# Moving a ring of four weight buffers by 64, 128, 192 and 256 bytes modulo 512 against the operand that streams through TensorE

## The chip, the cores and the metric

The kernel runs on one NeuronCore of one Trainium2 chip. The metric is the device time of one execution in microseconds. The kernel before took 2663.15 us as the median of two runs (2661.93 and 2664.38).

## What is computed

The input x is 8 sequences of 3008 tokens with 256 channels. Each sequence goes through a real Fourier transform along its tokens, a complex 256 x 256 mix of the channels, a soft threshold and the inverse transform; each token then goes through a gated feed-forward layer with 1536 hidden channels:

```python
X = np.fft.rfft(x, axis=1)
Yr = Xr @ w_r - Xi @ w_i + b_r
Yi = Xr @ w_i + Xi @ w_r + b_i
Y = soft(Yr, 0.01) + 1j * soft(Yi, 0.01)
x = np.fft.irfft(Y, n=3008, axis=1).reshape(8 * 3008, 256)
g = x @ w_gate
return (g / (1 + exp(-g)) * (x @ w_val)) @ w_out
```

## The kernel before

The work has two stages. The **transform stage** fills about the first 600 us: small matmuls (96x512, 128x128, 128x256, 128x512) compute the transforms and the mix, intermediate results go out to DRAM and come back, and the feed-forward weights are prepared and stored in DRAM. The **feed-forward stage** fills the rest. It runs over 24 blocks of tokens (22 of 2 x 512 tokens and 2 of 2 x 384), in each block over 6 pairs of hidden channels, and in each pair over gate and value: 24 x 6 x 2 = 288 steps, each a call of `gate_or_value`.

A step multiplies 2 x 2 blocks with seven products instead of eight (a Strassen-like scheme, with sums of blocks made by the other engines). Every operand is kept as two parts, an upper one rounded to fp32r and the rest, and `product` (L630 to L632) makes one product from three matmuls:

```python
for i, (w, x) in enumerate(((1, 0), (0, 0), (0, 1))):
    nc.tensor.matmul(o, lhsT=weights[w], rhs=parts[x], ...)
```

So one step has 7 x 3 = 21 matmuls of the "up" kind. Their stationary operand (lhsT, which TensorE loads before the matmul, the profile's LDWEIGHTS) is a 128 x 128 block of the step's weight unit `wup`, and their moving operand (rhs) is half of a tokens' part `x_parts`, 512 columns of 4 bytes in each partition. Among them stand "down" products of the pair before: the same `product`, with weights from `wdn_hi` and `wdn_lo`, which stay in SBUF throughout, and with `h_parts` as the moving operand. The order of the instructions of TensorE, VectorE, ScalarE and GpSimd is written out by hand in `gate_or_value`; on TensorE a run of 3, 6 or 9 "up" matmuls is followed by 3 "down" ones, over and over. In 32 steps `inverse` (L839 to L843) puts eight small fp32 matmuls in between, the end of the inverse transform of the last two sequences.

**The ring.** A weight unit has 2 x 7 x 128 floats in each partition (7168 bytes). `load_unit` (L586 to L590) takes the next of RING = 4 buffers of the pool `ring` and starts the DMA of a unit from DRAM on SP's queue; step k starts the load of unit k + 3 (L721). The pool is opened in `open_ring` (L582 to L584) at the right end of SBUF, behind a tile `pad` of PAD = 216 floats that nothing uses.

**Where the operands begin.** In this program the buffers of `wdn_hi`, `wdn_lo`, `x_parts` and `h_parts` all begin at 128 modulo 512 in each partition. A buffer of the ring takes 7168 = 14 x 512 bytes, and with the pad of 864 bytes above them all four ring buffers begin at 128 modulo 512 too (byte 199808, 206976, 214144 and 221312 of the partition). A block of weights is 512 bytes, a half of a tokens' part 2048. So for every matmul of the feed-forward stage the weights and the moving operand begin at the same place modulo 512. In the transform stage this differs: `f_hi` and `f_lo` begin 128 bytes above `wm_hi` and `wm_lo` modulo 512 (L366, L380), and `wi_hi` and `wi_lo` 128 bytes below `y_hi` and `y_lo` (L425).

Of the kernel before, what the change touches and what calls it, by code (L numbers as in the profile page):

```python
# [10 lines left out]
F32R = mybir.dt.float32r  # L11
# [6 lines left out]
P = 128  # L18
# [25 lines left out]
FIRST_X = {2: -0.93, 3: -0.90, 4: -0.5}  # L44
W_FIRST, W_STEP = 2, 4.2
WARM = 5
PAD = 216
GAPS = {1: (0.38,), 2: (0.38, 0.78), 3: (0.38, 0.78, 0.90), 4: (0.38, 0.40, 0.78, 0.90), 5: (0.36, 0.38, 0.40, 0.78, 0.90)}
AFTER = {0.36: 0.62, 0.38: 0.63, 0.40: 0.64, 0.78: 1.03, 0.90: 1.15}

# [59 lines left out]
def f32(ap):  # L110
    return ap.bitcast(F32)
# [458 lines left out]
class FFN:  # L570
# [11 lines left out]
    def open_ring(self):  # L582
        self.ctx.enter_context(self.tc.tile_pool(name="pad", bufs=1, side="right")).tile([P, PAD], F32, name="pad")
        self.ring = self.ctx.enter_context(self.tc.tile_pool(name="ring", bufs=RING, side="right", reuse_waits="tile"))  # L584

    def load_unit(self, k):  # L586
        if k >= len(BLOCKS) * len(self.units):
            return
        self.held[k] = self.ring.tile([P, 2, 7, P], F32R, name="wup")
        self.tc.nc.sync.dma_start(f32(self.held[k].rearrange("p i n a -> p i (n a)")), self.wup_d[self.units[k % len(self.units)]])  # L590

    def load_x(self, blk):
# [29 lines left out]
    def run(self, go, one):  # L622
        ctx, tc, front, ps_, co, wdn, d2, out = self.ctx, self.tc, self.front, self.ps_, self.co, self.wdn, self.d2, self.out
        xs, held, xt_d, load_unit, load_x, x_sum, x_part = self.xs, self.held, self.xt_d, self.load_unit, self.load_x, self.x_sum, self.x_part
        nc = tc.nc
        v, g, act = nc.vector, nc.gpsimd, nc.scalar
# [90 lines left out]
        def gate_or_value(pair, last, n, k, extra):  # L717

            blk, q, h = pair["blk"], pair["q"], pair["h"]
            x = xs[blk]  # L720
            load_unit(k + RING - 1)  # L721
            m5 = hidden[:, 4 + n, :h]
            first = last is not None and last["q"] == 0
# [251 lines left out]
```

## Time and profile before

| | |
|---|---|
| median of the runs | 2663.15 us |
| the profiled execution: time, span | 2661.2 us, 2659.1 us |
| TensorE matmul busy (PE) | 2632.8 us, 99% of the span |
| weight loads busy (PEld, beside the matmuls) | 2201.3 us, 83% |
| VectorE, ScalarE, GpSimd busy | 78%, 66%, 72% |
| granted TensorE clock, mean | 0.997 |
| loads of weight units | 288 of 896 KB, median 4.7 us from issue to landing |

The page's groups give for each line and engine the count, the busy time (overlaps counted once) and the mean duration of one instruction. A matmul's duration includes the time until its last result is written, so consecutive matmuls overlap and the duration is not what one costs: that is the distance from one start to the next, read from the timeline (start, length and count of each merged row) or from the chain of work (length and count of each piece). This distance is called the pitch below.

### The profile page before, as it was taken

To read this page: it belongs to the slowest core of one execution; us is meant where nothing else is said; L and a number is where in the kernel's file an instruction comes from. 1 tells how busy PE (TensorE), PEld (TensorE's weight loads), DVE (VectorE), ACT (ScalarE), POOL (GpSimd) and SP (SyncE) were. 2 spreads that over 40 slices of the span, in tenths; PEclk is the share of its full clock that TensorE was granted. 3 is DMA by queue.
4 is the path that set the end of the run, shared out by engine and by line. 5 is a ranking of instruction groups with operands and counts; after the bars stand their busy time and mean duration, and the time that the engine had idled before them with its cause. 6 is when DMAs were issued, how large, how long until landed. Compare 5 with 4: busy or idle time off the path is not lost.

```text
span 2659.1 us, 39894 instructions
## 1 busy us (share of the span) xinstructions
PE 2632.8 (99%) x13176; PEld 2201.3 (83%) x13176; DVE 2075.1 (78%) x3101; ACT 1742.5 (66%) x3374; POOL 1919.4 (72%) x1459
## 2 busy tenths in 40 slices
PE   8999999999999999999999999999999999999999
PEld 5787878997888888888888888888888888888899
DVE  4888887667877787777878787777778787888787
ACT  5887777776666666666665666666665666666665
POOL 1433333247888888888888888888888888888886
PEclk8999999999999999999999999999999999999999
DMA  9998988884544454445544544455445444444453
GB/s 281 309 302 283 291 267 248 268 263 142 165 157 155 166 170 162 155 150 172 168 157 154 171 163 159 144 171 168 157 149 175 161 145 140 167 157 153 154 174 126
DMA packets 184989, 493.04 MB, mean 185 GB/s; under 512 B 17776, under 2 KB 93680, under 8 KB 184688
## 3 DMA queue, kind: packets, MB, share of 16 engines
q1 hardware_dynamic: 184784, 490.50, 56.6%
q8 instruction: 105, 1.72, 0.3%
q14 instruction: 100, 0.82, 0.1%
HBM read 379.81 MB, written 110.62 MB: 184 GB/s over the span
## 4 chain that ended last, share of the span: by engine, by line
PE 92%; DVE 4%; ACT 2%; DMA 1%; issue 1%; SPq 0%; POOL 0%; DVEq 0%; ACTq 0%; POOLq 0%
PE bank L632 76%; PE mixb L380 3%; PE ps_a L305 3%; PE ps_x L450 3%; PE ps_b L327 2%; PE ps_z L425 2%; PE ps_s L366 2%; PE bank L843 1%; DVE f_hi L351 1%; DMA scratch<-xp 1%; DVE y_lo L412 1%; DVE f_lo L357 1%; ACT t L396 1%; DVE f_lo L354 0%; ACT f_hi L348 0%
## 5 line engine op out<-in xcount | busy, mean ns | idle before, releaser
L632 PE MATMUL bank<-x_parts,wup 128*128 128x512 f32 (+1 forms) x6048 | 1511.9, 385 | 0.3 <-DVE bank L767 0.2
L632 PEld LDWEIGHTS bank<-x_parts,wup 128*128 128x128 f32 x6048 | 1128.3, 188 | 222.5 <-DVE bank L767 1.8
L652 POOL TENSOR_TENSOR h_parts<-more,h_parts 128x512 fp32r<-128x512 f32 (+1 forms) x572 | 847.4, 1494 | 112.6 <-ACT h_parts L648 111.8
L652 POOL TENSOR_TENSOR h_parts<-hidden,h_parts 128x512 fp32r<-128x512 f32 (+1 forms) x431 | 561.8, 1311 | 207.5 <-ACT h_parts L648 195.2
L632 PE MATMUL bank<-h_parts,wdn_hi 128*128 128x512 f32 (+1 forms) x2014 | 612.3, 385 | 0.0
L648 ACT CAST h_parts<-hidden 128x512 fp32r<-128x512 f32 (+1 forms) x433 | 265.4, 613 | 455.8 <-DVE hidden L740 455.8
L673 DVE TENSOR_TENSOR sums<-sums,bank 128x512 f32<-128x512 f32 (+1 forms) x357 | 240.2, 673 | 255.0 <-PE bank L632 255.0
L740 DVE TENSOR_TENSOR hidden<-hidden,bank 128x512 f32<-128x512 f32 (+1 forms) x576 | 375.9, 674 | 78.2 <-PE bank L632 69.5
L632 PEld LDWEIGHTS bank<-h_parts,wdn_hi 128*128 128x128 f32 x2014 | 377.1, 188 | 71.6 <-POOL h_parts L652 0.5
L403 POOL TENSOR_TENSOR t<-t,y 128x512 f32<-128x512 f32 x96 | 122.4, 1275 | 385.3 <-DVE y L400 381.8
L632 PE MATMUL bank<-h_parts,wdn_lo 128*128 128x512 f32 (+1 forms) x1007 | 390.3, 388 | 0.0
L648 ACT CAST h_parts<-more 128x512 fp32r<-128x512 f32 (+1 forms) x572 | 349.9, 612 | 33.5 <-DVE more L643 22.6
L738 ACT ACTIVATE hidden<-bank 128x512 f32<-128x512 f32 (+1 forms) x432 | 252.1, 584 | 122.5 <-PE bank L632 114.2
L643 DVE TENSOR_TENSOR more<-hidden 128x512 f32<-128x512 f32 (+1 forms) x286 | 288.8, 1048 | 0.0
L643 DVE TENSOR_TENSOR more<-hidden,more 128x512 f32<-128x512 f32 (+1 forms) x286 | 255.3, 893 | 0.0
L745 ACT COPY bank<-bank 128x512 f32<-128x512 f32 (+1 forms) x288 | 161.6, 561 | 112.2 <-DVE hidden L740 103.6
L620 POOL TENSOR_TENSOR x_parts<-xf,x_parts 128x512 fp32r<-128x512 f32 (+1 forms) x168 | 210.6, 1272 | 23.1 <-ACT x_parts L619 21.4
L767 DVE TENSOR_TENSOR bank<-hidden,bank 128x512 f32<-128x512 f32 (+1 forms) x288 | 197.0, 684 | 38.0 <-PE bank L632 21.9
L632 PEld LDWEIGHTS bank<-h_parts,wdn_lo 128*128 128x128 f32 x1007 | 189.2, 188 | 34.9 <-DVE sums L673 0.2
L753 ACT COPY hidden<-bank 128x512 f32<-128x512 f32 (+1 forms) x288 | 167.5, 582 | 3.0 <-PE bank L632 0.4
L396 ACT COPY t<-mixb 64x256 f32<-64x256 f32 x384 | 140.7, 366 | 28.4 <-PE mixb L380 23.5
L380 PE MATMUL mixb<-wm_hi,f_hi 128*128 128x256 f32 x384 | 131.8, 343 | 1.4 <-DVE mixb L371 1.3
(102 smaller groups left out, 3054.1 us busy)
## 6 DMA issues: line engine op xcount, KB each, us to landing
wup<-wup_d SPq DMA_DIRECT2D x288, 896.0 KB, 4.7
d<-a SPq DMA_DIRECT2D x128, 192.0 KB, 3.8
a_in<-d SPq DMA_DIRECT2D x96, 256.0 KB, 4.9
d<-z SPq DMA_DIRECT2D x96, 256.0 KB, 4.8
out<-o SPq DMA_DIRECT2D x88, 256.0 KB, 6.2
scratch<-xp SPq DMA_DIRECT2D x116, 192.0 KB, 4.7
z_in<-d SPq DMA_DIRECT2D x48, 384.0 KB, 5.1
xt_d<-xt SPq DMA_DIRECT2D x48, 376.0 KB, 4.2
```

The costliest lines, as they stand in the source:

```text
L380: nc.tensor.matmul(mixed[p % 2][:, half * C : (half + 1) * C], lhsT=parts[x][:, q, cc, :], rhs=wmix[i][w][:, cc, :], start=False, stop=(cc ...
L396: act.copy(t[64 * half : 64 * half + 64, k * C : (k + 1) * C], mixed[p % 2][64 * k : 64 * k + 64, half * C : (half + 1) * C])
L620: self.tc.nc.gpsimd.tensor_tensor(part[:, 1, :h], src, f32(part[:, 0, :h]), op=ALU.subtract)
L632: nc.tensor.matmul(o, lhsT=weights[w], rhs=parts[x], start=start and i == 0, stop=stop and i == 2, skip_group_check=True)
L643: v.tensor_tensor(at(o, h), at(a, h), at(b, h), op=ALU.subtract)
L648: act.copy(pair[i][:, 0, :h], at(i, h))
L652: eng.tensor_tensor(pair[i][:, 1, :h], at(i, h), f32(pair[i][:, 0, :h]), op=ALU.subtract)
L673: v.tensor_tensor(o, o, spare[:, :h], op=ALU.add)
L738: act.activation(at(i, h), src, AF.Silu)
L740: v.tensor_tensor(at(i, h), at(i, h), src, op=ALU.mult)
L753: act.copy(m5, b2[:, :h])
L767: v.tensor_tensor(b2[:, :h], m5, b3[:, :h], op=ALU.add)
```

## The change

`PAD` goes from 216 to 136 floats (864 to 544 bytes), and each ring buffer is longer by SKEW = 16 floats (64 bytes), which nothing writes or reads. The ring's buffers begin at 192, 256, 320 and 384 modulo 512, that is 64, 128, 192 and 256 bytes above the moving operands. Pad and ring together are 64 bytes smaller; everything else stays where it was. Instructions, their order, sizes and shapes are the same. The DMA writes the same 7168 bytes in each partition.

```diff
-PAD = 216
+PAD = 136
+SKEW = 16
...
     def load_unit(self, k):
         if k >= len(BLOCKS) * len(self.units):
             return
-        self.held[k] = self.ring.tile([P, 2, 7, P], F32R, name="wup")
+        unit = self.ring.tile([P, 14 * P + SKEW], F32R, name="wup")
+        self.held[k] = unit[:, : 14 * P].rearrange("p (i n a) -> p i n a", i=2, n=7)
         self.tc.nc.sync.dma_start(f32(self.held[k].rearrange("p i n a -> p i (n a)")), self.wup_d[self.units[k % len(self.units)]])
```

## The prediction

> **What bounds the kernel now.** I read the page first, then the waits of TensorE's weight loads, then the chain of work by pieces, and last the timeline of single runs of matmuls.
>
> ```profile
> span 2659.1 us, 39894 instructions
> PE 2632.8 (99%) x13176; PEld 2201.3 (83%) x13176; DVE 2075.1 (78%) x3101; ACT 1742.5 (66%) x3374; POOL 1919.4 (72%) x1459
> PE 92%; DVE 4%; ACT 2%; DMA 1%; issue 1%; SPq 0%; POOL 0%; DVEq 0%; ACTq 0%; POOLq 0%
> L632 PE MATMUL bank<-x_parts,wup 128*128 128x512 f32 (+1 forms) x6048 | 1511.9, 385 | 0.3 <-DVE bank L767 0.2
> L632 PE MATMUL bank<-h_parts,wdn_hi 128*128 128x512 f32 (+1 forms) x2014 | 612.3, 385 | 0.0
> L632 PE MATMUL bank<-h_parts,wdn_lo 128*128 128x512 f32 (+1 forms) x1007 | 390.3, 388 | 0.0
> ```
>
> TensorE sets the end: the chain lies on it for 92%, and the three groups of L632 (6048 + 2014 + 1007 = 9069 matmuls) hardly wait. So every nanosecond that one of these matmuls gains or loses is in the total, and nothing else hides it. Between 640 and 2540 us the longest wait of the weight loads is this one, 1.0 us in total:
>
> ```profile
> PEld bank L632 <- DVE bank L767: 1.0, 5, 0.2
> ```
>
> The chain by pieces shows what one matmul costs there:
>
> ```profile
> 639.94 79.62 PE bank L632 x351
> 719.56 0.86 PE bank L843 x8
> 720.43 42.91 PE bank L632 x189
> ```
>
> 79.62 us / 351 = 226.8 ns, and 42.91 / 189 = 227.0 ns after an `inverse` (L843). The timeline is finer. It is read from start to start:
>
> ```profile
> 1501.34 2.20 PE L632 MATMUL bank<-x_parts,wup 128*128 128x512 f32 x9
> 1503.38 0.39 PE L632 MATMUL bank<-h_parts,wdn_lo 128*128 128x512 f32 x1
> ...
> 1505.42 2.20 PE L632 MATMUL bank<-x_parts,wup 128*128 128x512 f32 x9
> 1507.46 0.80 PE L843 MATMUL bank<-w,z 96*128 96x94 f32 x6
> ...
> 1508.27 0.47 PE L632 MATMUL bank<-h_parts,wdn_lo 128*128 128x512 f32 x1
> 1508.58 0.63 PE L632 MATMUL bank<-h_parts,wdn_hi 128*128 128x512 f32 x2
> 1509.05 2.23 PE L632 MATMUL bank<-x_parts,wup 128*128 128x512 f32 x9
> 1511.12 0.39 PE L632 MATMUL bank<-h_parts,wdn_lo 128*128 128x512 f32 x1
> ```
>
> Nine matmuls from 1501.34 to 1503.38 and nine from 1505.42 to 1507.46 take 2.04 us each time: **226.7 ns**. Behind the eight small matmuls of L843, the same instructions with the same operands take 1511.12 - 1508.58 = 2.54 us for eleven: **230.9 ns**. Nothing waits there. So the pitch has two levels at equal shapes: a settled one, and one that follows a disturbance and lasts some ten matmuls. (Check: 11 x 4.2 ns = 0.05 us over 189 matmuls is 0.25 ns each, which is about the difference of 227.0 to 226.8 above.)
>
> How much of the 226.7 ns is streaming comes from the blocks of 384 columns:
>
> ```profile
> 2573.59 0.33 PE L632 MATMUL bank<-h_parts,wdn_lo 128*128 128x384 f32 x1
> 2573.76 0.51 PE L632 MATMUL bank<-h_parts,wdn_hi 128*128 128x384 f32 x2
> 2574.11 0.68 PE L632 MATMUL bank<-x_parts,wup 128*128 128x384 f32 x3
> 2574.63 0.33 PE L632 MATMUL bank<-h_parts,wdn_lo 128*128 128x384 f32 x1
> 2574.80 0.51 PE L632 MATMUL bank<-h_parts,wdn_hi 128*128 128x384 f32 x2
> 2575.15 1.75 PE L632 MATMUL bank<-x_parts,wup 128*128 128x384 f32 x9
> ```
>
> Nine from 2573.59 to 2575.15 take 1.56 us, 173.3 ns. The 128 columns between the two shapes cost 53.4 ns, 0.417 ns a column; 512 columns are 213.6 ns, and **13.1 ns** of each matmul are something else. That is the only part that a shifted address can touch.
>
> **The change, part by part.** It removes and adds no instruction, no DMA and no wait, and moves no step past another. What it changes:
>
> *The load of a unit* writes the same bytes to other addresses. Its price I take as nothing, since it is covered: its landing takes 4.7 us (8.7 at most), and it is issued three steps ahead of its use, where a step has 21 + 10.5 matmuls x 0.2267 = 7.1 us. Even doubled landings stay inside 21 us.
>
> ```profile
> wup<-wup_d SPq DMA_DIRECT2D x288, 896.0 KB, 4.7
> DMA to landing us min/median/max: 4.3/4.7/8.7
> ```
>
> *The 6048 weight loads from the ring* read addresses that lie 64 to 256 bytes off the moving operand modulo 512; today it is 0 throughout the feed-forward stage. No matmul of 512 columns in that stage shows such a pair, so I bound the cost by rows of the transform stage. 128 bytes below, with 512 columns (L425):
>
> ```profile
> 211.96 0.39 PE L425 MATMUL ps_z<-y_hi,wi_hi 128*128 128x512 f32 x1
> 212.19 0.39 PE L425 MATMUL ps_z<-y_hi,wi_lo 128*128 128x512 f32 x1
> 212.42 0.40 PE L425 MATMUL ps_z<-y_lo,wi_hi 128*128 128x512 f32 x1
> 212.66 0.61 PE L327 MATMUL ps_b<-wf,a_in 128*128 128x128 f32 x4
> ```
>
> Three from 211.96 to 212.66, 233.3 ns each: 6.6 ns over the settled pitch, near the disturbed one. These three follow another kind of matmul, so they may be a disturbance and not a price of the offset. 128 bytes above, with 256 columns (L380), from the chain by pieces:
>
> ```profile
> 155.27 1.42 PE mixb L380 x12
> ```
>
> 1.42 us / 12 = 118.3 ns; less 256 x 0.417 = 106.8, 11.5 ns are left, which is 1.6 ns under the 13.1 of today. So the upper bound, if all 9069 matmuls ran like L425, is 9069 x 6.6 ns = +60 us; the lower bound, if 6048 had the remainder of L380, is 6048 x 1.6 = -10 us. The end of all gains is 6048 x 13.1 = -79 us, with no remainder left.
>
> Which value? The settled pitch is, as I read it, a rhythm between the reading of the next weights and of the moving operand: the same relation recurs at every matmul, and a disturbance dies out in ten. The change makes the relation alternate. Within a step the runs of 3, 6 or 9 ring matmuls (64 to 256 off) stand between triples from `wdn` (0 off), and the next step has another offset. Hardly any run is as long as the ten matmuls that settling took. So I expect the disturbed pitch, 230.9 ns, to stay: 4.2 ns more. For the 6048 "up" matmuls alone that is 25 us, for all 9069 it is 38 us. I take the middle, **+32 us**, as some triples and long runs will settle.
>
> *A rule against it.* The trace can't show how TensorE's two reads share SBUF; it shows only that equal shapes take 226.7 or 230.9 ns with no wait. The Trainium skill, TensorE: Matmul & The Clock Gate, Part 2, step 1 (LDWEIGHTS), says of the two read ports: "Loading the next tile's weights doesn't steal SBUF read bandwidth from the running matmul." By that rule no offset could matter, and the time would stay at 2661; the two levels at one shape speak against it, though they don't show that addresses are the cause. The same page, Back-to-back issue gap, has 512 / 2.4 + 2.5 = 215.8 ns for an isolated matmul; an estimate from it for ring matmuls with no conflict at all is 6048 x 10.9 ns = 66 us less, 2595.
>
> *The other engines* get slack if TensorE slows. If it sped up by 10 us of 2000, the busiest, GpSimd, would go from 83.2% to 83.6% of a stretch like the one below: no new bound.
>
> ```profile
> 1400.00:1600.00 200.00, 200.00 (x903) 166.25 (x902) 157.29 (x218) 126.32 (x228) 166.44 (x120) 1.00 0.50 161
> ```
>
> (The columns after the window are its length, then busy us and count of PE, PEld, DVE, ACT and POOL, the granted clock, the DMA share and GB/s.) The clock is fully granted and the stage stays as dense, so I expect no change there.
>
> **The sum.** The profiled execution took 2661.2 us (span 2659.1 and 2.1 around it), 0.07% under the median of 2663.15. 2661.2 + 0 for the loads + 32 = **2693 us**, +1.2%.
>
> **The rivals.**
>
> *Addresses don't matter* (or the rhythm settles at once at every offset). For it: the pitch is the same for `wup`, `wdn_hi` and `wdn_lo`, from buffers far apart. Against: all of them have offset 0, so the trace never tested it in this stage. Time: 2661.
>
> *The offset takes the conflict away*, the other side, so not slower. If at equal offsets both reads meet in the same part of the memory, and 64 to 256 bytes apart they pass each other, the ring matmuls lose part of their 13.1 ns. For it: L380, the one steady run with weights 128 bytes above, has 11.5. Against: L380 has half the columns, so its weight load fills nearly the whole matmul. Price by L380: -10 us, 2651. It beats my forecast's loss only if the ring's matmuls gain more than the `wdn` triples lose by being disturbed, 3021 x 4.2 = 13 us: from 2.1 ns a ring matmul on. To the end, all 13.1 ns, it is 2582.
>
> *The offset itself costs*, beyond the lost rhythm: all matmuls run like L425, +60 us, 2721. For it: 233.3 ns at 128 bytes below, and more than one of the four new offsets might be worse. Against: L425's triple comes right after another kind of matmul.
>
> **How the numbers follow.** Rhythm lost, +15 to +45 us: 0.45, with its own range 2676 to 2706. No effect: 0.2. Gain: 0.2, mostly small, 0.05 of it past 2%. The offset itself costs more than 45 us: 0.15, 0.12 of it past 2%. 2% is 53 us here, about what a measurement of this kernel can tell from no change; so faster 0.05, same 0.83, slower 0.12. The range reaches up to the bound by L425, 2721, and down to 2640, 21 us under the profiled execution, twice the gain by L380; under it I leave 0.1, over it 0.1.
>
> **What would show it.** Right: in the changed profile the pieces of the chain between two `inverse` take some 43.6 us for 189 matmuls instead of 42.91 (230.5 ns), the runs of nine take 2.07 to 2.10 us from start to start, and the 384-column blocks rise in the same way; no waits of PE appear, and landings stay near 4.7 us. If triples of `wdn` stay at 226.7 ns and only ring matmuls slow, the +25 end was right and the rhythm is not shared. If pieces stay at 42.91, addresses don't matter. If pitches fall below 226.7 ns for one or more of the four buffers, my reading of the settled state as the best one is wrong. If new waits or longer landings carry the difference, the step on the load was wrong.

## The result and the profile after

The changed kernel took **2689.32 us** (median of two runs, 2687.93 and 2690.72) against 2663.15: 1.010 times the kernel before, 95% interval 1.0083 to 1.0116. The profiled execution is the slower of the two, 2690.72 us. The forecast was 2693.

The page of the changed kernel, the lines that answer to those of before (L632 is now L634):

```profile
span 2688.6 us, 39894 instructions
PE 2660.6 (99%) x13176; PEld 2204.6 (82%) x13176; DVE 2064.7 (77%) x3101; ACT 1745.8 (65%) x3374; POOL 1917.2 (71%) x1459
PE 91%; DVE 4%; DMA 2%; ACT 2%; issue 1%; SPq 0%; POOL 0%; DVEq 0%; ACTq 0%; POOLq 0%
L634 PE MATMUL bank<-x_parts,wup 128*128 128x512 f32 (+1 forms) x6048 | 1531.7, 388 | 0.3 <-DVE bank L769 0.2
L634 PE MATMUL bank<-h_parts,wdn_hi 128*128 128x512 f32 (+1 forms) x2014 | 616.4, 387 | 0.0
wup<-wup_d SPq DMA_DIRECT2D x288, 896.0 KB, 4.7
```

The counts are the same, the idle time ahead of the matmuls is still 0.3 us, and a weight unit still lands in 4.7 us. What has grown is the busy time of TensorE, by 27.8 us. Where, the chain by pieces tells (start, length, what and count). First the kernel before, its unbroken stretch of matmuls from first piece to last:

```profile
613.04 32.11 PE bank L632 x140
...
2499.85 148.94 PE bank L632 x816
2648.78 0.02 issue
```

and the changed one:

```profile
616.05 29.12 PE bank L634 x125
...
2499.93 178.40 PE bank L634 x942
2678.32 0.02 issue
```

(Pieces at 2500 are cut by the window.) The stretch lasted 2648.78 - 613.04 = 2035.7 us and now lasts 2678.32 - 616.05 = 2062.3: **+26.5 us**. It begins 3.0 us later. These 3.0 us lie ahead of it, and may belong to this one execution: the other run of the changed kernel was 2.8 us faster in all. What follows the stretch is 10.3 us in both. So the change lies in the pitch of the feed-forward matmuls. A piece of 189 matmuls between two `inverse`, 42.91 us in the kernel before, now takes two lengths in turn:

```profile
725.04 43.40 PE bank L634 x189
...
769.30 43.63 PE bank L634 x189
```

The pitch is not the same in every step. The timeline of the changed kernel, one run of matmuls of each ring buffer, at 256, 192, 128 and 64 bytes above the moving operand in this order:

```profile
908.63 1.52 PE L634 MATMUL bank<-x_parts,wup 128*128 128x512 f32 x6
909.99 0.39 PE L634 MATMUL bank<-h_parts,wdn_lo 128*128 128x512 f32 x1
...
914.76 2.22 PE L634 MATMUL bank<-x_parts,wup 128*128 128x512 f32 x9
916.83 0.39 PE L634 MATMUL bank<-h_parts,wdn_lo 128*128 128x512 f32 x1
...
923.09 1.56 PE L634 MATMUL bank<-x_parts,wup 128*128 128x512 f32 x6
924.48 0.40 PE L634 MATMUL bank<-h_parts,wdn_lo 128*128 128x512 f32 x1
...
929.35 2.26 PE L634 MATMUL bank<-x_parts,wup 128*128 128x512 f32 x9
931.44 0.39 PE L634 MATMUL bank<-h_parts,wdn_lo 128*128 128x512 f32 x1
```

From start to start: 1.36 us for six at 256 (**226.7 ns**, as before), 2.07 for nine at 192 (230.0), 1.39 for six at 128 (231.7), 2.09 for nine at 64 (232.2). The starts of all matmuls of 512 columns in the trace, sorted by the ring buffer of their step, give means over the whole stage (a triple is three "down" matmuls; a pitch counts for the matmul that starts it):

| ring buffer at | ring matmuls, ns | wdn triples in its steps, ns |
|---|---|---|
| 0 (kernel before) | 226.9 | 226.8 |
| 64 | 233.0 | 231.8 |
| 128 | 232.4 | 231.3 |
| 192 | 229.4 | 226.7 |
| 256 | 227.6 | 226.8 |

The ring's matmuls together lose 20 us, the triples 6 us, and these 6 lie in the steps at 64 and 128, although the weights of a triple still begin where its moving operand does.

### The profile page after: what moved, and what is told of

Its sections match the earlier page's. It is cut to its first block, busy times and chain, and to the rows that moved or that the text cites. A ratio compares the mean times of both kernels' runs of the same rounds, so it can differ in the third digit from the quotient of the medians.

```text
span 2688.6 us, 39894 instructions
## 1 busy us (share of the span) xinstructions
PE 2660.6 (99%) x13176; PEld 2204.6 (82%) x13176; DVE 2064.7 (77%) x3101; ACT 1745.8 (65%) x3374; POOL 1917.2 (71%) x1459
## 4 chain that ended last, share of the span: by engine, by line
PE 91%; DVE 4%; DMA 2%; ACT 2%; issue 1%; SPq 0%; POOL 0%; DVEq 0%; ACTq 0%; POOLq 0%
PE bank L634 76%; PE mixb L381 3%; PE ps_a L306 3%; PE ps_b L328 2%; PE ps_x L451 2%; PE ps_z L426 2%; PE ps_s L367 2%; PE bank L845 1%; DVE f_hi L352 1%; DVE y_lo L413 1%; DVE f_lo L358 1%; ACT t L397 1%; DMA xt_d<-xt 0%; DMA d<-a 0%; ACT f_hi L349 0%
## 5 line engine op out<-in xcount | busy, mean ns | idle before, releaser
L634 PE MATMUL bank<-x_parts,wup 128*128 128x512 f32 (+1 forms) x6048 | 1531.7, 388 | 0.3 <-DVE bank L769 0.2
L634 PEld LDWEIGHTS bank<-x_parts,wup 128*128 128x128 f32 x6048 | 1129.8, 188 | 238.8 <-DVE bank L769 0.8
L654 POOL TENSOR_TENSOR h_parts<-hidden,h_parts 128x512 fp32r<-128x512 f32 (+1 forms) x431 | 555.8, 1295 | 226.4 <-DVE more L645 112.6
L634 PE MATMUL bank<-h_parts,wdn_hi 128*128 128x512 f32 (+1 forms) x2014 | 616.4, 387 | 0.0
L742 DVE TENSOR_TENSOR hidden<-hidden,bank 128x512 f32<-128x512 f32 (+1 forms) x576 | 376.0, 674 | 83.1 <-PE bank L634 71.7
L634 PEld LDWEIGHTS bank<-h_parts,wdn_hi 128*128 128x128 f32 x2014 | 377.3, 188 | 76.1 <-POOL h_parts L654 0.5
L634 PE MATMUL bank<-h_parts,wdn_lo 128*128 128x512 f32 (+1 forms) x1007 | 392.2, 390 | 0.0
L645 DVE TENSOR_TENSOR more<-hidden,more 128x512 f32<-128x512 f32 (+1 forms) x286 | 247.7, 866 | 0.0
L634 PEld LDWEIGHTS bank<-h_parts,wdn_lo 128*128 128x128 f32 x1007 | 189.3, 188 | 38.3 <-ACT h_parts L650 0.2
L792 DVE TENSOR_TENSOR hidden<-hidden,bank 128x512 f32<-128x512 f32 (+1 forms) x144 | 97.5, 677 | 52.9 <-PE bank L634 52.7
```

Source lines behind the costliest of these rows:

```text
L634: nc.tensor.matmul(o, lhsT=weights[w], rhs=parts[x], start=start and i == 0, stop=stop and i == 2, skip_group_check=True)
L645: v.tensor_tensor(at(o, h), at(a, h), at(b, h), op=ALU.subtract)
L654: eng.tensor_tensor(pair[i][:, 1, :h], at(i, h), f32(pair[i][:, 0, :h]), op=ALU.subtract)
L742: v.tensor_tensor(at(i, h), at(i, h), src, op=ALU.mult)
```

## The experiments

The sum was near, but these numbers fit the reason that the prediction gave for it only in part: at 256 almost nothing is lost. The theories at the start: **A**, every offset has a pitch of its own; **B**, the rhythm is lost because the offset alternates between ring (off) and `wdn` (0), the prediction's reason; **C**, only the differences between neighbouring ring buffers matter. In every kernel the profile shows the same counts and landings of 4.6 or 4.7 us; each is compared with runs of the kernel before on the same chip. For each kernel one line of its chain by pieces is shown, always a piece of 189 matmuls between two `inverse`; before it was 42.91 us.

**The ring at one offset.** The ring buffers as long as before, only the pad shorter:

```diff
-PAD = 216
+PAD = 200    # or 184, 168, 152: all four buffers 64, 128, 192, 256 bytes above
```

> All four ring buffers 64 bytes above the moving operands (pad 200 floats, no skew). Theory A, each offset has a pitch of its own, whatever stands next to it: in the changed kernel the matmuls of steps with offset 64 took 233.0 ns (ring) and 231.8 ns (wdn triples between them) against 226.9 and 226.8 before, so 6048 x 6.1 + 3021 x 5.0 ns = +52 us, 2715 us. Theory B, the rhythm is lost because the offset alternates between ring and wdn matmuls, whatever the offset is: as much as the changed kernel lost, +26 us, 2689 us. Theory C, only the different offsets of neighbouring ring buffers disturb: no change, 2663 us.

2709.66 us, ratio 1.0181 (1.0166 to 1.0196), +48 us.

```profile
723.98 43.99 PE bank L634 x189
```

> All four ring buffers 128 bytes above (pad 184 floats, no skew). Theory A: 232.4 ns (ring) and 231.3 ns (wdn) in the changed kernel's steps of this offset, so 6048 x 5.5 + 3021 x 4.4 ns = +47 us, 2710 us. Theory B: 2689 us. Theory C: 2663 us.

2705.39 us, ratio 1.0166 (1.0151 to 1.0181), +44 us.

```profile
723.66 43.92 PE bank L634 x189
```

> All four ring buffers 192 bytes above (pad 168 floats, no skew). Theory A: 229.4 ns (ring), 226.7 ns (wdn), so 6048 x 2.5 ns = +15 us, 2678 us. Theory B: 2689 us. Theory C: 2663 us.

2694.33 us, ratio 1.0124 (1.0107 to 1.0141), +33 us.

```profile
722.47 43.70 PE bank L634 x189
```

> All four ring buffers 256 bytes above (pad 152 floats, no skew). Theory A: 227.6 ns (ring, the settling after the offset before included) and 226.8 ns (wdn) in the changed kernel, settled 226.7: 0 to +4 us, 2663 to 2667 us. Theory B: 2689 us, since the ring stands 256 bytes off and wdn 0. Theory C: 2663 us.

2662.69 us, ratio 1.0002 (0.9992 to 1.0011), no change.

```profile
718.87 42.91 PE bank L634 x189
```

Theory C falls: three of the four are slow with no difference between buffers. Theory B in this form falls too: at 256 the ring alternates with `wdn` at 0 just as at 64, and the pitch is that of before. Theory A gives the differences at 64, 128 and 256 within 4 us. At 192 it missed, 33 us instead of 15. There the triples show why. In the changed kernel the triple behind the run at 914.76 took 226 ns a matmul, and all triples of that buffer 226.7 on average; with the ring at 192 throughout, the timeline has

```profile
906.05 0.40 PE L634 MATMUL bank<-h_parts,wdn_lo 128*128 128x512 f32 x1
906.28 0.63 PE L634 MATMUL bank<-h_parts,wdn_hi 128*128 128x512 f32 x2
906.74 1.54 PE L634 MATMUL bank<-x_parts,wup 128*128 128x512 f32 x6
908.13 0.40 PE L634 MATMUL bank<-h_parts,wdn_lo 128*128 128x512 f32 x1
```

three in 0.69 us (230 ns), and 231.6 as a mean over all triples. The same offsets thus run at two speeds, so what stands around them counts: in the changed kernel the steps at 192 follow the settled ones at 256. So a second form of B stayed open, that switching between offsets that differ modulo 256 costs.

**No alternation.** A tile that nothing uses, set into the pool of the resident weights, moves the later buffers on the left of SBUF. Behind `w21` it moves `x_parts` and `h_parts` up by 64 bytes (all weights 64 below them, 192 modulo 256):

```diff
     w21 = const.tile([P, 2, P], F32R, name="w21")
+    const.tile([P, 16], F32, name="shift")
```

> The kernel before with a tile of 16 floats behind the resident weights, so that x_parts and h_parts begin 64 bytes higher while wdn and the ring stay: all 9069 matmuls have their weights 64 bytes below the moving operand (192 modulo 256), with no alternation. Theory A, the offset itself costs: all matmuls at the 230.2 to 231.6 ns of the kernel with the ring at 192, 9069 x 3.4 to 4.7 ns = +31 to +43 us, 2693 to 2705 us. Theory B in its second form, a pitch is lost only where offsets alternate that differ modulo 256 (ring against wdn): no alternation is left, so 2663 us.

2680.34 us, ratio 1.0071 (1.0056 to 1.0086), +18 us.

```profile
721.40 43.31 PE bank L633 x189
```

Neither theory has it. Without any alternation the offset costs, so B in its second form falls as the whole cause; but 9069 matmuls at 192 cost little more than half of what 6048 did with the ring alone, so there the switching adds at least 14 us (an estimate: 20 us, if the ring's 6048 matmuls alone would cost two thirds of 18). From one start to the next the pitches in the trace repeat 226, 229, 232 ns without end, a mean of 229.0: not a disturbance that dies out but a steady cycle.

With the tile ahead of `wdn`, of 16 or 32 floats, a second one of 112 or 96 floats behind `w21`, and PAD at 200 or 184, all weights stand 64 or 128 above and the moving operands stay:

```diff
+    const.tile([P, 16], F32, name="shift")
     wdn = [const.tile([P, NQ, 7, P], F32R, name=f"wdn_{p}") for p in ("hi", "lo")]
     w21 = const.tile([P, 2, P], F32R, name="w21")
+    const.tile([P, 112], F32, name="back")
```

> All 9069 matmuls have their weights 64 bytes above the moving operand (wdn and ring 64 bytes higher, x_parts and h_parts back at 128 by a second tile). Theory D, an offset has its own steady cycle, and the triples at offset 0 only cut it short: in the long runs of the kernel with the ring at 64 the pitch alternates 231 and 236 ns, 233.5, so 9069 x 6.7 ns = +61 us, 2723 us, with triples as slow as the ring. Theory E, the switching between ring and wdn is the larger part, as it is at 192 (33 us with it, 18 without): less than with the ring alone, some +26 us, 2688 us.

2714.31 us, ratio 1.0201 (1.0185 to 1.0216), +52 us.

```profile
723.59 44.12 PE bank L634 x189
```

> The same at 128 bytes above. Theory D: the long runs of the kernel with the ring at 128 alternate 237 or 238 and 229 ns, 233.4, so 9069 x 6.6 = +60 us, 2722 us. Theory E: less than the +44 us with the ring alone, some +24 us, 2686 us.

2712.77 us, ratio 1.0191 (1.0176 to 1.0207), +51 us.

```profile
724.81 44.12 PE bank L634 x189
```

Theory D holds and E falls: 44.12 / 189 = 233.4 ns, the pitch that D took from the long runs, and triples as slow as the ring. In time it came out some 9 us below D's 61 and 60, because D priced the 384-column blocks like the rest: by the starts in the trace (without the few over 220 ns) those rose only from 174.6 to 175.4 and 176.3 ns, and 8316 matmuls of 512 columns x 6.4 ns are 53 us. The more matmuls at 64 or 128, the slower. Still, the triples at 0 were only a small relief: with the ring alone at 64 they took 231.3 ns, against 233.3 here and 226.8 in the kernel before.

**Only the relation, or the place?** The 16-float tile ahead of `wdn`, none behind, PAD = 200: everything 64 bytes higher, all offsets 0.

> The kernel before with a tile of 16 floats ahead of the resident weights and the pad 16 floats shorter: wdn, ring, x_parts and h_parts all begin 64 bytes higher, at 192 modulo 512, so every offset is 0 again. If only the relation between weights and moving operand counts (theories A and B): 2663 us. If the place itself counts (a buffer should begin at 128 modulo 512): as with the ring at 64, +48 us or more, 2710 us.

2661.21 us, ratio 0.9999 (0.9989 to 1.0008).

```profile
723.91 42.91 PE bank L633 x189
```

The ring stands at the same bytes here as in the kernel with the ring at 64, which lost 48 us. The place doesn't matter, the relation does.

**`wdn` alone off.** The tile of 16 floats behind `w21` and PAD = 200: the ring at 0, `wdn` 64 below.

> wdn alone 64 bytes below the moving operands, ring at offset 0 (x_parts, h_parts and ring 64 bytes higher). Theory A with a memory of ten matmuls: 3021 matmuls with a bad offset, and the ring's runs of 3, 6 or 9 between them never settle: between 3021 x 3.4 = +10 us and 9069 x 4.7 = +43 us; if the ring's matmuls have their own pitch at once, only +10 to +14 us, 2673 to 2677 us; if the triples disturb all, 2690 us or more. Theory B in its second form: alternating, so as slow as the ring at 192 alone, +33 us, 2694 us.

2667.48 us, ratio 1.0023 (1.0014 to 1.0032), +5.5 us, less than any theory said.

```profile
720.87 43.03 PE bank L633 x189
```

The timeline shows the ring settled at once:

```profile
901.84 0.39 PE L633 MATMUL bank<-h_parts,wdn_lo 128*128 128x512 f32 x1
902.07 0.62 PE L633 MATMUL bank<-h_parts,wdn_hi 128*128 128x512 f32 x2
902.53 1.52 PE L633 MATMUL bank<-x_parts,wup 128*128 128x512 f32 x6
903.89 0.39 PE L633 MATMUL bank<-h_parts,wdn_lo 128*128 128x512 f32 x1
```

The triple takes 0.69 us (230 ns each), the six ring matmuls behind it 1.36 us, 226.7 ns each. So not every switch is followed by ten matmuls of settling. The reverse case differs: with the ring off, the triples at 0 were slowed, as the table and the timeline at 192 show.

**Smaller steps, and the period.** Ring at 32 (PAD = 208), at 224 (PAD = 160), and buffers 256 bytes longer in place of 64 (SKEW = 64, PAD = 24):

> All four ring buffers 32 bytes above (pad 208 floats, no skew). If the reads meet in lines of 64 bytes, an offset within the line is as good as 0: 2663 us. If any offset other than 0 modulo 256 costs: between the ring at 192 and at 64, +33 to +48 us, 2694 to 2710 us. If a small offset moves the conflict out of the way, below 226.7 ns: under 2655 us.

2703.17 us, ratio 1.0157 (1.0140 to 1.0174), +41 us.

```profile
723.63 43.86 PE bank L632 x189
```

> All four ring buffers 224 bytes above, which is 32 below modulo 256 (pad 160 floats, no skew). If below is cheaper than above, as 192 is than 64: less than the +41 us of the ring at 32, some +10 to +30 us, 2673 to 2693 us. If only the distance from 0 modulo 256 counts: as the ring at 32, 2703 us. If the two reads miss each other best just below: under 2655 us.

2703.98 us, ratio 1.0158 (1.0141 to 1.0175), +42 us: 32 below is as bad as 32 above, and no offset that was tried is better than 0.

```profile
723.28 43.87 PE bank L632 x189
```

> Ring buffers 256 bytes longer instead of 64 (skew 64 floats, pad 24): they stand at 256, 0, 256 and 0 above the moving operands. If the place counts modulo 256 only: 2663 us, pitch 226.7 in every step. If a change of offset from one buffer to the next costs by itself: settling of about ten matmuls with 4.2 ns at each of 288 steps, +13 us, 2676 us.

2661.30 us, ratio 0.9996 (0.9986 to 1.0005).

```profile
720.66 42.91 PE bank L634 x189
```

Skewed buffers as such cost nothing: with a step of 256 bytes they alternate between 256 and 0 and run as before.

## Why the prediction came out right, and where its reason was wrong

- *What bounds the kernel* held. TensorE's feed-forward matmuls stand back to back in both kernels, and each nanosecond of their pitch is in the total: +26.5 us of the profiled execution's +29.5, the rest lying ahead of the stretch. The granted clock is 1.00 from 640 to 2540 us in both.
- *The load of a unit at nothing* held: 4.7 us to landing, and no new wait.
- *+32 us* was measured as +26.5 in the stage. The mechanism of this step failed, "Hardly any run is as long as the ten matmuls that settling took. So I expect the disturbed pitch, 230.9 ns, to stay". Alternation alone costs nothing: the ring at 256 against `wdn` at 0 runs as before, and with `wdn` alone off the ring keeps its 226.7 ns. All weights at 64 or 128 with no alternation cost the most (+52, +51). What costs is the offset modulo 256: a steady cycle of pitches, 226.7 ns at 0, 229.0 at 192, 233.4 at 64 and 128.
- A part of the reason held: where the ring is off, it can slow the triples beside it, whose own offset is 0. Of the +26.5 us some 6 are theirs, 5 ns a matmul in the steps at 64 and 128 and nothing in those at 192 and 256. With the ring alone at 64, 128 or 192 the triples took 231.1 to 231.6 ns, some 12 us in all, and the pitches between two matmuls of one triple rose too, to 230.5 ns at 64 and 231.3 at 192.
- *The signs.* The pieces take 43.40 and 43.63 us (43.6 was expected) and runs of nine 2.07 and 2.09. The triples answer neither way, since they slow in two buffers' steps and stay in the other two. The 384-column blocks did not rise in the same way: from 174.6 to 175.6 ns, against 226.9 to 230.1 for 512 columns.
- That the sum came so near is in good part luck. The mean pitch of 230.1 ns is the mix of one buffer that lost almost nothing and three that lost 2.5 to 6.1 ns on their own account; it isn't one disturbed pitch of 230.9 in all steps.
- The third rival, the offset itself, came nearest. It was given 2721 and a chance of 0.15, as it was priced with all matmuls like L425. The four offsets dilute it. The ring at one offset cost 48, 44, 33 and 1 us; their mean is 31. The changed kernel stayed some 5 under it, mostly because the triples of its steps at 192 keep 226.7 ns instead of 231.6: 4.9 ns x 3021 / 4 = 4 us.
- *The two rows that bounded the cost.* L425 (128 below, 233.3 ns) was set aside as perhaps a disturbance. Its number is that of all weights at 128 (233.4; 128 below is 128 above modulo 256), but the row doesn't show which of the two it is: in the kernel before, the second to fourth matmul behind each `inverse`, all at offset 0, take 229, 233 and 236 ns, and L425's three have medians of 229.5, 233 and 234. L380 (128 above, 256 columns, 11.5 ns left over) was the wrong row: at the same offset 512 columns leave 233.4 - 213.6 = 19.8. A remainder found at one column count doesn't hold at another.
- *Addresses don't matter*: falls, except between 0 and 256. The Trainium skill's sentence on the two read ports (TensorE: Matmul & The Clock Gate, Part 2, step 1), as the prediction applied it, would have put every kernel here at 2661; the offset alone makes up to 2.0%.
- *The gain*: none at any offset tried. The 13.1 ns beside the streaming stayed at 0 and grew elsewhere.

## What to carry to other kernels

Where a chain of weight loads and 512-column fp32r matmuls bounds a kernel, try to let stationary and moving operands begin at the same place modulo 256 bytes; here it cost nothing to arrange, and up to 2% to miss. Look at the start-to-start pitch of equal matmuls before calling them equal: two levels with no wait between them are a sign, as they were here, that something beside the shape counts. To find out what, vary one placement for all buffers at once and sort the starts by buffer; a mix of four placements shows a mean that fits a wrong reason as well as the right one.

## What the runs showed of the hardware that was not expected

- The pitch of a 512-column matmul with its weight load depends on where the weights begin against the moving operand: settled 226.7 ns at 0 and 256, cycles of 226, 229, 232 at 192, of 229 and 238 at 128, and at 64 either of 231 and 236 or of 233, 233, 234, with nearly the same mean. With the ring alone at 32 and 224 it costs 41 and 42 us. 256 bytes are the smallest step shown to be free; offsets that are not multiples of 32 were not tried, nor were 96 and 160.
- A matmul's pitch also depends on the matmuls around it: the same triples took 226.7 or 231.6 ns in steps with the ring at 192, with the neighbouring steps at 256 and 128 or at 192 too. And behind each of the 32 `inverse` between 640 and 2500 us of the kernel before, the second to the tenth matmul, all at offset 0, take 231.2 ns on average before 226.7 returns, with no wait.
- With 384 columns the offset costs little: 0.8 and 1.7 ns with all weights at 64 and 128, where 512 columns lose 6.4.
- Why this is so stays open. That the reading of the next weights and of the moving operand meet in the memory would fit a cost that goes by their relation, but no run shows the reads themselves, and it doesn't say why 64 and 192 differ, why a ring that is off slows its neighbours, or why 13.1 ns remain at the best offsets.
